# The passage from the filter stage to the first token tile: store position, last frequency pairs, and the order and banks at the first last stage

## Chip, cores and metric

The kernel runs on one core of one Trainium2 chip, as one launch. The metric is the device time of that launch in microseconds (us); lower is better. Times given as positions ("at 294.16") are microseconds from the start of the span of one profiled execution.

## What is computed

The reference is a long convolution with a small learned filter, a gate, and a maxout feed-forward layer on the result:

```python
h_mlp = np.maximum(pos_emb @ w1, 0.0) @ w2            # 12544 x 128, filter
h_filt = h_mlp * exp(-0.01 * pos)
u = x * v                                              # 4 x 12544 x 128
y = irfft(rfft(u, 2S) * rfft(h_filt, 2S), 2S)[:, :S]   # per channel
a = (x * y).reshape(50176, 128)
h = maximum(maximum(a @ w1m, a @ w2m), a @ w3m)        # 128 -> 768
out = h @ w_out                                        # 768 -> 128
```

All arrays are float32 on the chip (the feed-forward weights arrive as 64-bit floats and are converted there). There are B = 4 samples of S = 12544 positions and D = 128 channels.

## The kernel before

**Transforms as products.** A sequence of 12544 positions is seen as 98 blocks (NB) of 128. The Fourier transform of each channel is done in two stages of small matrix products. The first stage works on "units": a unit is four channels, and there are 32 of them per sample. `u_first` multiplies a unit's turned data by a table (32 matmuls, line 413), ScalarE copies one half of the result out of PSUM into a buffer `high` (line 422), and VectorE writes sum and difference of the two halves into `spec` (line 424). The second stage works on 45 "pairs" of frequencies (NK = 45, pairs 0 to 44): a product with the second table, a multiplication by the filter's spectrum, and the product of the inverse transform, whose result goes to DRAM (`zd`).

**Token tiles.** The rest of the inverse transform runs tile by tile. A tile is four block positions, 392 tokens; a sample has 32 tiles (NT). `t_load` brings a tile's data back from `zd` to `zt` and the matching x to `xT`; `t_sums` makes sum and difference of its halves (line 703); `t_last` does the last product (32 small matmuls through line 156) and VectorE multiplies by x into `gt` (line 724). Then for six blocks of 128 hidden units `up` does two products into a ring of three PSUM banks called `hbanks`, ScalarE applies relu (line 734), VectorE takes the maximum (line 737), and `down` accumulates the output product two steps later. The third maxout branch was folded into the other two beforehand; the fold product is `lin` (line 1085 copies it out).

**Order.** The program order of every engine is written out by hand: each engine and each DMA queue works its own list in order, and the framework adds the waits that buffers and data need. SyncE's queue issues nearly all loads; POOL (GpSimd) issues the stores of the filter and of the output.

**The stage before the passage** is the loop at line 1038 over s, from 0 to 47. In one turn it starts pair s, makes the filter of pair s-1 (`s_filter`, lines 1007 and 1012: a product, and a copy into a buffer `ht`, of which there are two), stores it for later samples (`s_store`, line 1018: two DMAs on POOL's queue), multiplies pair s-2 by its filter and makes sum and difference for the inverse product (`g_re`, `g_im`, `g_unfold`: lines 549, 553, 554, 561), and does the inverse product of pair s-3 (`g_third`, stored by line 574). At s = NK two pairs, 43 and 44, are handled in one turn: both are multiplied, then both unfolded, and the add of pair 43 is on POOL (`apart`).

**The passage.** Units 0 to 5 of the second sample (unit 0 at s = 45, unit 1 behind the loop, units 4 and 5 only turned there) use PSUM banks of the stage that is ending; `banks_of` lists them in order. Behind the loop the fold products run (`folding`), `lin` is copied out, the old pools are closed, and the new ones open: three banks of the up ring, two double banks `cps` for everything else ("pairs" in the code), one bank for the output. The first tile of sample 0 then runs in this order: loads of tiles 0 and 1, `t_sums` of tile 0 on VectorE, `u_first(2)`, `t_last` of tile 0, `u_first(3)`, and the first `up`. From there the products of the second sample's transform are put between the tiles' products, by slots that a planner (`conv_steps`) assigns.

Of the kernel before, what the change touches and what calls it, by code (L numbers as in the profile page):

```python
# [10 lines left out]
FP32 = mybir.dt.float32  # L11
I32 = mybir.dt.int32
U16 = mybir.dt.uint16
ALU = mybir.AluOpType
ACTF = mybir.ActivationFunctionType
PSUM = bass.MemoryType.PSUM
P = 128
# [74 lines left out]
def kernel(  # L92
# [15 lines left out]
    nc = tc.nc  # L108
    NG, _, _, B, NB = x.shape
# [4 lines left out]
    NK = N1 // 2  # L114
# [286 lines left out]
                t[0:NB, 4 * h:4 * h + 4].rearrange("n s p -> n (s p)").rearrange(  # L401
                    "n (s t r) -> n s r t", s=8, r=2))

    def u_first(u, i0=0, n=4):


        t = uts[u] if i0 + n < 4 else uts.pop(u)
        ps = state["bank"]()[:, 0:256 * n]
        at = 4 * u + i0
        for i in range(n):  # L410
            for h in range(2):
                for c in range(2):
                    nc.tensor.matmul(  # L413
                        ps[64 * c:64 * c + 64, 256 * i + h * N1:256 * i + (h + 1) * N1],
                        t[:, 2 * ((at + i) % 8) + h].rearrange("n r t -> n (r t)"),
                        f1q[:, h, c * N1:(c + 1) * N1],
                        start=(i % 2 == 0 and h == 0), stop=True, skip_group_check=True)
        v = ps.rearrange("p (s m) -> p s m", m=256)[:, :, 0:2 * N1].rearrange(
            "p s (h k) -> p h k s", h=2)
        high = cvp.tile([P, n, D], FP32, tag="eo", name="high", bufs=2)  # L420
        high = high[:, :, 0:N1].rearrange("p s k -> p k s")
        nc.scalar.copy(high, v[:, 0])  # L422
        for a, op in enumerate((ALU.add, ALU.subtract)):
            nc.vector.tensor_tensor(out=spec[:, :, a, at:at + n], in0=v[:, 1], in1=high, op=op)  # L424

    def w_load(x):
        w = wp.tile([P, 2, 2, 2, 64], FP32, tag="w", name="wt")
# [123 lines left out]
    def g_im(g, apart=False):  # L551
        xt, xs = xts[g], xss.pop(g)
        nc.vector.tensor_tensor(out=xs[:], in0=xs[:], in1=hts.pop(g)[:, 1], op=ALU.mult)
        (nc.gpsimd if apart else nc.vector).tensor_tensor(
            out=xt[:], in0=xt[:], in1=xs[:], op=ALU.add)
# [112 lines left out]
    def t_load(b, i):  # L668
        zt = hp.tile([N1, 2, 512], FP32, tag="zt", name="zt", bufs=2)
        for c in range(2):  # L670
            if b == 0:
                nc.sync.dma_start(
                    zt[NK * c:NK * c + NK],
                    zd[b].rearrange("(g a) c t f -> g a c t f", a=2)[
                        :, :, c, 2 * i:2 * i + 2, :].rearrange("g a t f -> g a (t f)"))
                continue
            q, j = divmod(i, NT // 2)
            for a in range(2):
                nc.sync.dma_start(
                    zt[NK * c:NK * c + NK, a].rearrange("g (t f) -> g t f", t=2),  # L680
                    zd[b].rearrange("(g a) c t q f -> g a c t q f", a=2)[
                        :, a, c ^ (a & q), 2 * j:2 * j + 2, q, :])
        zts[b, i] = zt[:, 0], zt[:, 1]
        if i % 2:
            return
        xT = hp.tile([D, 2, 4, NB], FP32, tag="xT", name="xT", bufs=2)
        for c in range(GC):
            nc.sync.dma_start(xT[c * NG:(c + 1) * NG].rearrange("d i p n -> d (i p) n"),
                              x[:, 4 * i:4 * i + 8, c, b, :])
        xTs[b, i], xTs[b, i + 1] = xT[:, 0], xT[:, 1]  # L690
# [3 lines left out]
    def t_sums(i, eng=nc.gpsimd, parts=(0, 1)):  # L694
        z0, z1 = zts[i]
        if 0 in parts:
            evens_[i] = hp.tile([N1, 512], FP32, tag="even", name="even", bufs=2)
        even = evens_[i]
        for a, (out, op) in enumerate(((even[:], ALU.add), (z1, ALU.subtract))):
            if a not in parts:  # L700
                continue
            if i[0] == 0 or i[1] < NT // 2:
                eng.tensor_tensor(out=out, in0=z0, in1=z1, op=op)
            else:
                nc.vector.scalar_tensor_tensor(out=out, in0=z1, scalar=sign_t[:, 0:1], in1=z0,
                                               op0=ALU.mult, op1=op)
        if 1 in parts:
            zts[i] = evens_.pop(i)[:], z1

    def t_last(i):  # L710
        zt = zts.pop(i)
        ps = state["bank"]()
        own = i[0] == B - 1 and i[1] > 1
        g = (lp if own else hp).tile([D, 4, NB], FP32, tag="g", name="gt", bufs=4 if own else 3)
        y = ps[:, 0:N].rearrange("d (p n) -> d p n", p=4)

        h = NB // 2
        for s in range(4):
            for a in range(2):
                halves_mm(y[:, s, a * h:a * h + h], zt[a][:, s * D:(s + 1) * D],  # L720
                          f4p[:, i[0] > 0 and i[1] >= NT // 2, a, :], s == 0 and a == 0, True)
        y = y.rearrange("d p (a m) -> d p m a", a=2)
        xT = xTs.pop(i)
        nc.vector.tensor_tensor(out=g[:].rearrange("d p (m a) -> d p m a", a=2), in0=y,
                                in1=xT.rearrange("d p (m a) -> d p m a", a=2),
                                op=ALU.mult)
        gs[i] = g
# [180 lines left out]
    for f in range(0, FO, 4):  # L908
        quad([hs[:, f + i] for i in range(4)], (f1h[:, 0], f1h[:, 1]), specH[:, :, :, f:f + 4])
        u, k = divmod(f // 4, 4)  # L910
# [36 lines left out]
    gps = pro.enter_context(tc.tile_pool(name="gps", bufs=2, space=PSUM))  # L947
    sps = pro.enter_context(tc.tile_pool(name="sps", bufs=1, space=PSUM))
    def banks_of():
        for _ in range(2):  # L950
            yield gps.tile([P, 512], FP32, tag="g", name="ps1")[:]
        both = sps.tile([P, 1024], FP32, tag="h", name="ps1")
        for h in range(2):
            yield both[:, 512 * h:512 * h + 512]
        for pool, tag in ((cps, "cv"), (gps, "g")):
            yield pool.tile([P, 512], FP32, tag=tag, name="pst")

    free = banks_of()

# [56 lines left out]
    def s_store(g):  # L1016
        for c in range(2):
            nc.gpsimd.dma_start(
                hd[g, 64 * c:64 * c + 64],
                hts[g][64 * c:64 * c + 64, c].rearrange("p k q d -> p (k q d)"))  # L1020
# [17 lines left out]
    for s in range(NK + 3):  # L1038
        if s < NK:
            ws[s, 0] = wf[s]  # L1040
            s_second(s)
            if s + 1 < NK:
                s_minus(s + 1)
            g_second(s)
            wf.pop(s)
            if s + 3 < NK:
                wf[s + 3] = load_dir(s + 3, 0)
        if 1 <= s <= NK:
            g_swap(s - 1)
            s_filter(s - 1)  # L1050
        if s >= 3:
            ws[s - 3, 1] = wi.pop(s - 3)
            g_third(s - 3)
            if s < NK:
                wi[s] = load_dir(s, 1)
        ready = [g for g in {NK: (s - 2, s - 1)}.get(s, (s - 2,)) if 0 <= g and s <= NK]
        for g in ready:
            s_store(g)
            g_re(g)
            g_im(g, g == NK - 2)  # L1060
        for g in ready:
            g_unfold(g)
        if s < NK:
            g_butterfly(s)

        if s in muls:
            u_mul(muls[s])
        if s in turns:
            u_turn(turns[s])
        if s in loads:  # L1070
            u_load(1, loads[s])
        if s == NK:
            unit(0)
            pl = sps.tile([P, 512], FP32, tag="pl", name="pl")
        if s == NK + 1:
            for f in range(2):
                folding(f)
# [40 lines left out]
    for n, (b, i) in enumerate(tiles[:LAST]):  # L1118
        if i == 0:
            plan, pairs_from = plans[b]  # L1120
        if n == 0:
            t_load(*tiles[0])
            t_load(*tiles[1])
            t_sums(tiles[0], nc.vector)
            u_first(2)
            t_last(tiles[0])
            u_first(3)
        for f in range(NF):

            if i < NT - 2:  # L1130
                if f == 0:
                    t_load(*tiles[n + 2])
            elif i == NT - 1 and f < 2 and n + 1 + f < len(tiles):
                t_load(*tiles[n + 1 + f])
            turn_ = i == NT - 1
            if f == 4 and n + 1 == LAST:
                t_sums(tiles[n + 2], nc.vector)
            h = up((b, i), f)
            for a in range(2):
                if f == plan[i][a]:  # L1140
                    t_sums(tiles[n + 1],
                           nc.vector if turn_ or i * NF > pairs_from else nc.gpsimd, (a,))
            late.append(((b, i), f, h))
            if len(late) > 2:
                down(*late.pop(0))
            if f == plan[i][2]:
                t_last(tiles[n + 1])
            if f == 5 and n + 1 == LAST:
                t_last(tiles[n + 2])
            run(besides.pop(n * NF + f, ()))  # L1150
# [97 lines left out]
```

## Time and profile before

| | |
|---|---|
| median of three runs | 2289.66 us (2287.26 to 2293.03) |
| the profiled execution | 2287.31 us, span 2285.5 us |
| TensorE (PE) busy | 2258.4 us, 99% |
| VectorE (DVE) busy | 1558.0 us, 68% |
| ScalarE (ACT) busy | 1173.6 us, 51% |
| GpSimd (POOL) busy | 871.6 us, 38% |
| mean granted TensorE clock | 0.997 |
| first `up` product of tile 0 | 313.67 us |

The profile is of one execution on the chip. PE is TensorE's matmuls, PEld its weight loads; SPq and POOLq are the queues in which SyncE and GpSimd issue DMAs. A busy share over the whole span mixes stages with different limits, so the passage, some 30 us near position 300, is read by itself below.

### The profile page before, as it was taken

The numbers are of one execution on the slowest core, as the hardware profiler recorded it, in microseconds if no ns is written. First come the engines' busy times: TensorE is split into PE (matmuls) and PEld (weight loads), VectorE is DVE, ScalarE is ACT, GpSimd is POOL, SyncE is SP. The second block draws the span as 40 slices with busy tenths as digits, with TensorE's granted clock in tenths as the row PEclk, the third lists the DMA queues.
The fourth block names the chain that finished last, engine by engine and source line by source line (L and its number), as shares of the span: only waits on it lengthen the run. The fifth ranks groups of instructions, "written<-read, shape, count | busy, mean of one in ns | idle before, by whom it ended". The sixth has DMA issues, their size and how long they took to land.

```text
span 2285.5 us, 68501 instructions
## 1 busy us (share of the span) xinstructions
PE 2258.4 (99%) x27855; PEld 1381.6 (60%) x27855; DVE 1558.0 (68%) x2853; ACT 1173.6 (51%) x2124; POOL 871.6 (38%) x1088
## 2 busy tenths in 40 slices
PE   8999989999999999999999999999999999999998
PEld 7988866655555556655555556655555546666665
DVE  5588956667788757657878756667878854544443
ACT  2688844456666534456666534456666622222222
POOL 2044424323332333423333334413333326666666
PEclk9999999999999999999999999999999999999999
DMA  7778979799989779879999789879999832222221
GB/s 188 182 233 271 302 169 179 147 216 241 237 220 241 190 169 177 162 182 254 238 232 240 207 162 188 155 183 246 233 239 237 204 86 56 56 67 65 62 56 22
DMA packets 473270, 411.03 MB, mean 180 GB/s; under 512 B 327866, under 2 KB 374427, under 8 KB 472955
## 3 DMA queue, kind: packets, MB, share of 16 engines
q1 hardware_dynamic: 445954, 329.48, 63.8%
q0 software_dynamic: 26288, 75.47, 11.1%
q8 instruction: 219, 3.59, 0.7%
q10 hardware_dynamic: 712, 1.70, 0.3%
q14 instruction: 97, 0.79, 0.1%
HBM read 262.84 MB, written 84.67 MB: 152 GB/s over the span
## 4 chain that ended last, share of the span: by engine, by line
PE 96%; DMA 2%; DVE 1%; issue 1%; ACT 0%; SPq 0%; POOL 0%; POOLq 0%; DVEq 0%; ACTq 0%
PE hps L156 44%; PE ops L156 19%; PE ops L797 6%; PE cps L413 5%; PE cps L156 4%; PE ps L156 3%; PE cps L467 3%; PE ps L165 3%; PE cps L477 3%; PE sps L1007 2%; PE gps L989 2%; PE last L156 1%; DMA hd<-ht 1%; PE pst L366 1%; PE pm L328 1%
## 5 line engine op out<-in xcount | busy, mean ns | idle before, releaser
L156 PE MATMUL hps<-gt,w_sb 128*64 128x392 f32 x6144 | 1150.4, 494 | 0.0
L734 ACT ACTIVATE hid<-hps 128x392 f32<-128x392 f32 x768 | 383.7, 500 | 697.6 <-PE hps L156 680.8
L156 PEld LDWEIGHTS hps<-gt,w_sb 128*64 128x64 f32 x6144 | 432.6, 137 | 419.6 <-issue 384.0
L737 DVE TENSOR_TENSOR hid<-hid,hps 128x392 f32<-128x392 f32 x768 | 427.8, 557 | 332.4 <-PE hps L156 322.2
L156 PE MATMUL ops<-hid,wo_sb 128*64 128x392 f32 x2304 | 480.5, 492 | 0.0
L519 POOL TENSOR_TENSOR cb<-cb,xs 128x512 f32<-128x512 f32 x135 | 173.6, 1286 | 463.4 <-DVE xs L516 346.1
L156 PEld LDWEIGHTS ops<-hid,wo_sb 128*64 128x64 f32 x2304 | 172.8, 137 | 206.4 <-issue 197.8
L424 DVE TENSOR_TENSOR spec<-cps,high 128x360 f32<-128x360 f32 x188 | 141.0, 790 | 127.8 <-ACT high L422 127.0
L492 DVE TENSOR_TENSOR cb<-cps,eo 128x512 f32<-128x512 f32 (+1 forms) x288 | 175.1, 649 | 73.9 <-ACT eo L489 73.9
L752 POOL DMA_DIRECT2D out_dram<-ot x96 | 75.1, 783 | 345.5 <-ACT ot L750 298.0
L507 ACT ACTIVATE xs<-cb 32x512 f32<-32x512 f32 x270 | 169.5, 628 | 20.4 <-DVE cb L492 11.5
L422 ACT COPY high<-cps 128x360 f32<-128x360 f32 x94 | 75.0, 798 | 182.5 <-PE cps L413 149.1
L508 ACT COPY xs<-cb 32x512 f32<-32x512 f32 x270 | 166.3, 616 | 3.2
L413 PEld LDWEIGHTS cps<-f1q,uT 98*64 98x64 f32 x3008 | 131.9, 138 | 29.8 <-issue 23.8
L523 DVE TENSOR_TENSOR xs<-cb 128x256 f32<-128x256 f32 x270 | 140.8, 566 | 9.1 <-POOL cb L519 8.9
L413 PE MATMUL cps<-f1q,uT 98*64 98x90 f32 x3008 | 136.3, 242 | 3.2 <-DVE uT L397 1.5
L382 POOL COPY planes<-ut 128x784 uint16<-128x784 uint16 x90 | 76.4, 849 | 153.5 <-DVE ut L361 153.5
L500 POOL DMA_DIRECT2D zd<-cb x135 | 92.5, 685 | 64.5 <-DVE cb L492 56.9
L156 PEld LDWEIGHTS cps<-f4p,even 90*64 90x64 f32 x1568 | 90.8, 138 | 34.8 <-issue 32.8
L156 PE MATMUL cps<-f4p,zt 90*64 90x49 f32 x1568 | 97.4, 222 | 0.1
L821 POOL DMA_DIRECT2D out_dram<-o x128 | 77.4, 610 | 49.6 <-DVE o L814 47.9
L156 PE MATMUL cps<-f4p,even 90*64 90x49 f32 x1568 | 96.1, 220 | 0.0
(135 smaller groups left out, 3140.6 us busy)
## 6 DMA issues: line engine op xcount, KB each, us to landing
ht<-hd SPq DMA_DIRECT2D x264, 256.0 KB, 6.9
wt<-wq_const SPq DMA_DIRECT2D x144, 256.0 KB, 6.3
zd<-cb POOLq DMA_DIRECT2D x135, 256.0 KB, 6.1
zt<-zd SPq DMA_DIRECT2D x384, 90.0 KB, 3.1
sq<-spec SPq DMA_DIRECT2D x264, 128.0 KB, 7.0
ut<-in_xr_dram SPq DMA_DIRECT2D x128, 196.0 KB, 3.9
ut<-in_vr_dram SPq DMA_DIRECT2D x128, 196.0 KB, 4.1
xT<-in_x_dram SPq DMA_DIRECT2D x256, 98.0 KB, 3.3
```

The lines of the kernel that those rows point to most:

```text
L156: nc.tensor.matmul(out[64 * h:64 * h + 64], lhsT[:, 64 * h:64 * h + 64], rhs, start=start, stop=stop, skip_group_check=True)
L413: nc.tensor.matmul(ps[64 * c:64 * c + 64, 256 * i + h * N1:256 * i + (h + 1) * N1], t[:, 2 * ((at + i) % 8) + h].rearrange("n r t -> n (r ...
L424: nc.vector.tensor_tensor(out=spec[:, :, a, at:at + n], in0=v[:, 1], in1=high, op=op)
L492: nc.vector.tensor_tensor(out=cb[:, a, lo:hi], in0=ps[:, lo:hi], in1=eo[:, lo:hi], op=op)
L500: nc.gpsimd.dma_start(zd[b][2 * z:2 * z + 2].rearrange("k c t a f -> (k c t) a f"), zss.pop(z))
L507: nc.scalar.mul(xs[at:at + 32], xt[at + 32:at + 64], -1.0)
L508: nc.scalar.copy(xs[at + 32:at + 64], xt[at:at + 32])
L519: nc.gpsimd.tensor_tensor(out=xts[g], in0=xts[g], in1=xs[:], op=ALU.add)
L523: nc.vector.tensor_tensor(out=ab[:, q], in0=y[:, 0], in1=y[:, 1], op=(ALU.subtract, ALU.add)[q])
L734: nc.scalar.activation(h[:], pa[:, 0:N], Relu)
L737: nc.vector.tensor_tensor(out=h[:], in0=h[:], in1=pb[:, 0:N], op=ALU.max)
L797: nc.tensor.matmul(ps[64 * c:64 * c + 64, 0:H2], w, rhs[:, H2 * c:H2 * c + H2], start=start, stop=True, skip_group_check=True)
```

## The change

Four things are altered; the work computed is the same.

- The stores of filters 42 and 43 are issued one turn of the loop sooner: at s = 43 those of 41 and 42, at s = 44 that of 43, at s = 45 that of 44.
- At s = 45 pair 43 is multiplied, added and unfolded, and then pair 44; both adds are on VectorE.
- The list of banks gives unit 1's two halves two different tiles (the filter's double tile and one of the two `gps` banks) instead of two halves of one tile.
- `u_first` is split into `u_products` (products and the copy to `high`) and the two VectorE operations that it returns as a function. At tile 0 the order becomes: loads, unit 2 whole, products of unit 3, `t_sums`, `t_last` in the next bank of the up ring, and then unit 3's two VectorE operations.

```diff
-    def u_first(u, i0=0, n=4):
+    def u_products(u, i0=0, n=4):
...
         nc.scalar.copy(high, v[:, 0])
-        for a, op in enumerate((ALU.add, ALU.subtract)):
-            nc.vector.tensor_tensor(out=spec[:, :, a, at:at + n], in0=v[:, 1], in1=high, op=op)
+
+        def both():
+            for a, op in enumerate((ALU.add, ALU.subtract)):
+                nc.vector.tensor_tensor(out=spec[:, :, a, at:at + n], in0=v[:, 1], in1=high,
+                                        op=op)
+        return both
+
+    def u_first(*args):
+        u_products(*args)()
...
-    def t_last(i):
+    def t_last(i, bank=None):
         zt = zts.pop(i)
-        ps = state["bank"]()
+        ps = bank or state["bank"]()
...
     def banks_of():
-        for _ in range(2):
-            yield gps.tile([P, 512], FP32, tag="g", name="ps1")[:]
-        both = sps.tile([P, 1024], FP32, tag="h", name="ps1")
-        for h in range(2):
-            yield both[:, 512 * h:512 * h + 512]
-        for pool, tag in ((cps, "cv"), (gps, "g")):
-            yield pool.tile([P, 512], FP32, tag=tag, name="pst")
+        for pool, tag, n in ((gps, "g", 1), (gps, "g", 1), (sps, "h", 2), (gps, "g", 1),
+                             (cps, "cv", 1), (gps, "g", 1)):
+            yield pool.tile([P, 512 * n], FP32, tag=tag, name="ps1")[:, 0:512]
...
         ready = [g for g in {NK: (s - 2, s - 1)}.get(s, (s - 2,)) if 0 <= g and s <= NK]
+        for g in {NK - 2: (s - 2, s - 1), NK - 1: (s - 1,), NK: (s - 1,)}.get(s, (s - 2,)):
+            if 0 <= g and s <= NK:
+                s_store(g)
         for g in ready:
-            s_store(g)
             g_re(g)
-            g_im(g, g == NK - 2)
-        for g in ready:
+            g_im(g)
             g_unfold(g)
...
             t_load(*tiles[1])
+            u_first(2)
+            third = u_products(3)
             t_sums(tiles[0], nc.vector)
-            u_first(2)
-            t_last(tiles[0])
-            u_first(3)
+            t_last(tiles[0], next(hbanks))
+            third()
```

## Prediction

> **What bounds the kernel now.** I read the busy shares first. TensorE is busy 2258.4 of 2285.5 us, so only about 27 us of the span are TensorE idle. The mean granted clock is 0.997. Then I asked for TensorE's waits. From 320 to 1850 us they sum to 1.5 us, so a change can pay only in the start, in the passage from the filter stage to the first token tile, or at the end. The diff touches the passage. From 287 to 315 us TensorE is busy 20.67 of 28 us at a mean clock of 0.82. The timeline of TensorE, cut to the instructions that waited there (start, length, instruction, in brackets the idle time before it and what ended it):
>
> ```profile
> 287.67 1.10 PE L1007 MATMUL sps<-w2x,G 64*64 64x128 f32 x32 [0.79 <-ACT ht L1012]
> ...
> 294.16 1.97 PE L156 MATMUL ps<-ab,wt 128*64 128x128 f32 x16 [3.12 <-DVE ab L561]
> ...
> 301.97 0.84 PE L413 MATMUL ps<-f1q,uT 98*64 98x90 f32 x16 [1.34 <-DVE spec L424]
> ...
> 307.02 1.46 PE L413 MATMUL cps<-f1q,uT 98*64 98x90 f32 x32 [0.36 <-ACT lin L1085]
> ...
> 311.06 2.61 PE L413 MATMUL cps<-f1q,uT 98*64 98x90 f32 x32 [1.38 <-DVE spec L424]
> ```
>
> In order: the last filter product; inverse product of pair 43; second half of unit 1; unit 2; unit 3. Sixteen 128-wide matmuls take 1.09 us at 288.70 but 1.97 us at 294.16, and unit 3 takes 2.61 us against unit 2's 1.46: the clock. By windows (columns: window, length, then busy time and count of PE, PEld, DVE, ACT and POOL, then granted clock, DMA share, GB/s):
>
> ```profile
> 294.00:301.00 7.00, 6.20 (x54) 5.15 (x54) 2.59 (x9) 1.79 (x5) 0.00 (x0) 0.51 0.28 92
> ...
> 311.00:315.00 4.00, 3.94 (x39) 3.16 (x41) 0.87 (x2) 0.90 (x2) 2.48 (x3) 0.57 0.67 153
> ```
>
> Next, why pair 43 waited. VectorE, then POOL:
>
> ```profile
> 288.26 0.68 DVE L553 TENSOR_TENSOR xs<-xs,ht 128x512 f32<-128x512 f32 x1
> 291.75 0.69 DVE L549 TENSOR_TENSOR xt<-xt,ht 128x512 f32<-128x512 f32 x1 [2.81 <-ACT ht L1012]
> ...
> 293.69 1.42 DVE L561 TENSOR_TENSOR ab<-xt 128x256 f32<-128x256 f32 x4
> ```
>
> ```profile
> 284.10 1.04 POOL L1018 DMA_DIRECT2D hd<-ht  x2 [2.06 <-ACT ht L1012]
> 287.91 1.05 POOL L1018 DMA_DIRECT2D hd<-ht  x2 [2.77 <-ACT ht L1012]
> 289.03 1.27 POOL L554 TENSOR_TENSOR xt<-xt,xs 128x512 f32<-128x512 f32 x1
> ```
>
> Pair 43 has its filter at 287.65. Its sum is done on POOL at 290.30, but VectorE unfolds it only at 293.69, behind all of pair 44. Pair 44 waits for a filter buffer: the copy at 290.70 had to wait until the store of filter 42 landed. The chain of waits (start, length, what):
>
> ```profile
> 284.61 5.99 DMA hd<-ht
> ...
> 290.70 1.02 ACT ht L1012
> ...
> 300.13 2.18 DMA zd<-zs
> ```
>
> From 300.13 the chain goes on through the store of the last inverse result, its reload (landed 307.15) and the sums to the first up product at 313.67.
>
> **What the Trainium skill says.** "TensorE: Matmul & The Clock Gate", Part 1, has the array at half clock after an idle window of about 3.4 us, back at full after a busy one, with windows that run freely. The trace agrees: 3.12 us idle, then clock 0.50 until after 300.6 us. "PSUM — Partial Sum Buffer", section on bank collisions, says to guard PSUM by bank. Unit 1's halves lie in different banks but in one tile, and the second waits 1.34 us for the first's readers: here the wait comes from the tile, and two tiles remove it. "DMA: Bandwidth & Descriptors", Anatomy of one DMA, gives about 2.0 us of fixed cost; the lone store at 300.13 took 2.2 us, so an earlier issue moves it whole.
>
> **The change, part by part.**
>
> 1. Stores. Those of filters 42 and 43 move an iteration up: four DMA issues of 0.53 us on POOL's queue, passing nothing there, since POOL's last other step (the negation at 280.10) stays ahead. Both began 0.30 us after the copy they need (283.80 to 284.10, 287.61 to 287.91), with POOL idle before. So nothing is won; filter 44 is still copied at 290.70. Nothing lost either.
>
> 2. Last pairs. POOL's add (1.27) goes, VectorE's (0.69) comes, and pair 43 is unfolded before pair 44 begins. VectorE is idle from 288.94 to 291.75, which covers it: add 288.97 to 289.66, unfold to 290.45. TensorE ends unit 0 at 291.04, so pair 43 runs at once: 3.12 us of wait gone. Late next is pair 44: multiplies and add 291.75 to 293.76 unchanged, its unfold now first, 293.79 to 294.50. Between lie two transposes and a fold product, about 1.0 us. Pair 44's product goes from 294.2 and ends at **T' = 295.3** at full clock or 296.1 at half, where before T = 299.43. Its output buffer is free when the store of 292.23 lands (3.2 us: 295.4), about when it is needed. Gain at T: 3.3 to 4.1 us.
>
> 3. Banks. Unit 1's second half goes to another tile, freed by unit 0's adds (about 295.5): 1.34 us gone. The folding from unit 1's end (302.81) to the end of `lin` (306.97) keeps its 4.16 us. So **L'** = T' + 1.41 + 4.16 = 300.9 at full clock; at half, T' + 2.82 + 4.16 = 303.1.
>
> 4. Order at tile 0. Unit 3's product follows unit 2's; the last stage stands in a bank of the up products, so it waits for no adds of unit 2; unit 3's adds follow. But on VectorE unit 2's two adds now stand ahead of the tile's sums; before, the sums filled the wait for unit 2's copy. From L': copy of unit 2 starts at +1.67, its adds end at +3.95 (as before), sums (0.69 + 0.69) at +5.35, last stage ends 1.08 later as it did (308.61 to 309.69), product with x 0.56: first up product at **U' = L' + 7.15**. The reload, landing 7.7 us after T', is no longer last: 303.0 against adds that end at 304.9. Before, U was L + 6.70, with 1.15 of clock in unit 3. So this part gives back 0.45, or 1.6 at equal clocks.
>
> Sum: full clock, U' = 308.05 against 313.67, 5.6 us; half, 310.25, 3.4 us. The quiet stretch from L' + 2.8 to U' holds only 1.3 us of TensorE work, so half clock after it is as likely as not: up to 1.7 us (half of a window that the page puts at 3.4; before, the up products lost 0.5). That takes 0.35 on average. I weigh the clocks 55 to 45: 0.55 x 5.2 + 0.45 x 3.0 = 4.2; **4.3 us** taken, as the sums could move up if the clock is full. The extremes of this case are 2.2 and 6.1.
>
> 5. Later. One more bank in the up ring turns it by one place: nothing, since each up still takes the next of three. Unit 3's adds (1.49) after the first product with x hold a pair bank and a copy buffer not needed before unit 5. The ring's first banks are free by then. But the last stage now ends 0.75 us ahead of U', where it ended 4.0 ahead of U; its end frees the buffer for tile 2's load, and behind that load on SP's queue stand four x loads and eight unit loads. VectorE's multiply of unit 7 needs data that landed 10.3 us after the last stage's end: now U' + 9.6, done at U' + 10.2. TensorE waits only from about U' + 11.0 (the maximum of the fourth up product has 1.8 us in hand). Costed at nothing, by 0.8 us.
>
> The profiled execution took 2287.31 us around its span of 2285.5; the median of the three runs is 2289.66. Taking 4.3 off each gives 2283.0 and **2285.4**.
>
> **Rivals.** *Supply binds* (0.15): the SP queue above. In absolute time the last stage ends only 0.2 to 2.4 us sooner (307.3 to 309.5 against 309.69). If the loads pace TensorE, the gain is that, 2288. For: DMA share near 1.0 from 315 on. Against: no engine waited for a unit load before. *Clock stays full* (0.15): gain 6.1 at most against the profiled execution, and up to 8 against the median, which stands 2.35 above it: 2282 to 2284. *The clock stays low from 292 to past the first ups* (0.10), the other side: idle 292.5 to 293.75 triggers it, and folding with many transposes fails to lift it. L' = 294.2 + 1.97 + 2.82 + 6.5 (its 3.3 us of work doubled, 0.9 waits) = 305.5, unit 2 adds 1.2, U' = 313.9 and the ups lose 1.2 more: 1.4 us slower, 2291. It decides where the clock between 292 and 308 falls under about 0.6. *The change does nothing in its first part*: argued above, inside every case. The forecast has 0.60.
>
> **Numbers.** Runs of this kernel differ by 5.8 us among three, and 0.3% is 6.9 us, about what can be told from no change. The range 2281.5 to 2289.5 takes in the forecast's extremes, supply and most of the full-clock case. Faster by over 0.3% needs a median under 2282.8: half of the full-clock case and a share of the forecast's, 0.18. Slower by over 0.3% needs something not seen here: 0.03.
>
> **What would show it.** Right: pair 43's product at about 291.0 without a wait; no wait in unit 1; the stores still 0.3 us after their copies; filter 44's copy near 290.7; unit 2's adds ahead of the sums; the first up near 308 to 311. Wrong: a filter copy or store that moved by over 1 us; a wait of VectorE for unit loads near 315 followed by TensorE waits; a sum of TensorE's waits after 320 above 3 us.

## The result

The changed kernel takes 2284.69 us in the median of 22 runs (2281.04 to 2287.29), the kernel before 2289.15 in 22 runs beside them: 4.46 us less. The ratio is 0.998, 95% interval 0.9974 to 0.9987, that is 3.0 to 6.0 us. The forecast was 2285.4. The gain is within the 0.3% that the forecast called no change, but clear of noise. One execution of a later set of 20, at 3354 us and a clock of 0.654, is left out of every figure below.

The profiled execution of the changed kernel has by chance the same span as that of before, 2285.5 us: at 2287.29 us it is the slowest of its 22, while that of before, 2287.31, lies 1.8 us under its median. Its stages ahead of the passage ran 3.2 us later, so positions of the two traces can't be compared as they stand. I count from a mark ahead of every edit but the stores': **F**, the start of the last filter product (287.67 before, 290.91 after). The stores of filters 42 and 43 stand where they stood from F: 3.57 us ahead of it and 0.24 behind it, in both traces. TensorE after the change, mostly its waits (start, length, instruction, idle before and what ended it; L156 is the line of a helper, and the trace counts each float32 matmul of the program as two):

```profile
290.91 1.10 PE L1010 MATMUL sps<-w2x,G 64*64 64x128 f32 x32 [0.79 <-ACT ht L1015]
...
296.76 0.44 PE L156 MATMUL pl<-wo_sb,w1t 128*64 128x128 f32 x4 [0.88 <-ACT w1t L974]
297.61 1.17 PE L156 MATMUL ps<-ab,wt 128*64 128x128 f32 x16 [0.40 <-issue]
298.60 1.41 PE L413 MATMUL ps<-f1q,uT 98*64 98x90 f32 x32
...
304.22 2.70 PE L413 MATMUL cps<-f1q,uT 98*64 98x90 f32 x64 [0.36 <-ACT lin L1089]
308.78 0.32 PE L156 MATMUL hps<-f4p,even 90*64 90x49 f32 x4 [1.85 <-DVE even L710]
309.50 0.32 PE L156 MATMUL hps<-f4p,zt 90*64 90x49 f32 x4 [0.40 <-DVE zt L710]
...
311.19 2.88 PE L156 MATMUL hps<-gt,w_sb 128*64 128x392 f32 x8 [0.67 <-DVE gt L731]
...
320.72 1.41 PE L413 MATMUL cps<-f1q,uT 98*64 98x90 f32 x32
```

The first up product and unit 5's products in the kernel before:

```profile
313.39 2.11 PE L156 MATMUL hps<-gt,w_sb 128*64 128x392 f32 x8
...
320.50 1.44 PE L413 MATMUL cps<-f1q,uT 98*64 98x90 f32 x32
```

The 3.12 us ahead of pair 43 and the 1.34 us inside unit 1 (298.60, now 32 matmuls in one piece) are gone. The first up product starts at F + 20.28, where it started at F + 25.72. (The 313.67 of the table before, F + 26.0, is the end of the products ahead of it; its first matmul starts at 313.39.) But it now takes 2.88 us for 8 matmuls that take 1.54 in the fill kernel below, at full clock. By windows (length, busy time and count of PE, PEld, DVE, ACT, POOL, then the granted clock, DMA share, GB/s):

```profile
294.00:310.00 16.00, 11.85 (x194) 9.07 (x192) 8.16 (x18) 8.12 (x19) 1.05 (x2) 1.00 0.62 161
310.00:318.00 8.00, 7.33 (x66) 4.55 (x64) 3.10 (x5) 1.65 (x3) 2.76 (x3) 0.57 0.72 169
```

The half clock of 294 to 301 is gone; that behind the first last stage has grown from 3.4 to 6.8 us. VectorE and POOL:

```profile
292.22 0.69 DVE L561 TENSOR_TENSOR xt<-xt,xs 128x512 f32<-128x512 f32 x1
293.01 0.76 DVE L568 TENSOR_TENSOR ab<-xt 128x256 f32<-128x256 f32 x2
294.95 0.69 DVE L556 TENSOR_TENSOR xt<-xt,ht 128x512 f32<-128x512 f32 x1 [1.18 <-ACT ht L1015]
...
306.69 1.44 DVE L426 TENSOR_TENSOR spec<-cps,high 128x360 f32<-128x360 f32 x2 [5.46 <-ACT high L422]
308.04 0.68 DVE L710 TENSOR_TENSOR even<-zt 90x512 f32<-90x512 f32 x1
```

```profile
287.34 1.05 POOL L1021 DMA_DIRECT2D hd<-ht  x2 [2.37 <-ACT ht L1015]
291.15 1.05 POOL L1021 DMA_DIRECT2D hd<-ht  x2 [2.76 <-ACT ht L1015]
295.21 1.05 POOL L1021 DMA_DIRECT2D hd<-ht  x2 [3.02 <-ACT ht L1015]
```

Pair 43 is unfolded (293.01) before pair 44 has its filter (294.95). The sums (308.04) begin when unit 2's adds end. The chain of waits shows what pair 43 hangs on now:

```profile
288.01 6.27 DMA wt<-wt_const
294.29 0.14 issue
294.42 1.09 PE ps L156 x16
```

Its inverse table landed 0.14 us before it ran. In run 7, where no load stands in the chain ahead of it, the product starts 1.25 us after the start of unit 0's products; here it is 1.55.

### The profile page after: what moved, and what is told of

Read it like the earlier page. It is cut to its first block, busy times and chain, and to the rows that moved or that the text cites. A ratio compares the mean times of both kernels' runs of the same rounds, so it can differ in the third digit from the quotient of the medians.

```text
span 2285.5 us, 68498 instructions
## 1 busy us (share of the span) xinstructions
PE 2258.2 (99%) x27855; PEld 1376.8 (60%) x27855; DVE 1558.6 (68%) x2854; ACT 1175.3 (51%) x2124; POOL 871.8 (38%) x1087
## 4 chain that ended last, share of the span: by engine, by line
PE 96%; DMA 1%; DVE 1%; ACT 1%; issue 0%; POOL 0%; POOLq 0%; ACTq 0%; DVEq 0%; SPq 0%
PE hps L156 44%; PE ops L156 19%; PE ops L804 6%; PE cps L413 5%; PE cps L156 4%; PE cps L474 3%; PE ps L156 3%; PE ps L165 3%; PE cps L484 3%; PE sps L1010 2%; PE gps L992 1%; PE last L156 1%; DMA hd<-ht 1%; PE pst L366 1%; PE pm L328 1%; PE pw L156 1%
## 5 line engine op out<-in xcount | busy, mean ns | idle before, releaser
L156 PE MATMUL hps<-gt,w_sb 128*64 128x392 f32 x6144 | 1151.1, 495 | 0.7 <-DVE gt L731 0.7
L156 PEld LDWEIGHTS hps<-gt,w_sb 128*64 128x64 f32 x6144 | 430.9, 137 | 422.3 <-issue 393.4
L156 PE MATMUL ops<-hid,wo_sb 128*64 128x392 f32 x2304 | 479.9, 492 | 0.0
L156 PEld LDWEIGHTS ops<-hid,wo_sb 128*64 128x64 f32 x2304 | 171.8, 137 | 207.4 <-issue 207.4
L413 PEld LDWEIGHTS cps<-f1q,uT 98*64 98x64 f32 x3008 | 131.4, 138 | 29.3 <-issue 26.5
L156 PEld LDWEIGHTS cps<-f4p,even 90*64 90x64 f32 x1552 | 89.6, 138 | 35.0 <-issue 34.2
L156 PE MATMUL cps<-f4p,zt 90*64 90x49 f32 x1552 | 96.3, 222 | 0.0
L156 PE MATMUL cps<-f4p,even 90*64 90x49 f32 x1552 | 95.0, 220 | 0.0
```

The costliest lines, as they stand in the source:

```text
L156: nc.tensor.matmul(out[64 * h:64 * h + 64], lhsT[:, 64 * h:64 * h + 64], rhs, start=start, stop=stop, skip_group_check=True)
L413: nc.tensor.matmul(ps[64 * c:64 * c + 64, 256 * i + h * N1:256 * i + (h + 1) * N1], t[:, 2 * ((at + i) % 8) + h].rearrange("n r t -> n (r ...
```

## Experiments

**How they are read.** For each trace I give the passage, from F to the start of unit 5's products (line 413; from 320 to 1850 us TensorE waits 1.5 us in all, before and after), and the rest of the span behind it. "Half clock" is the time at half clock from the first last stage on: twice the shortfall of the granted clock, summed over windows of 1 us.

| kernel | F | unit 5 | passage | half clock | rest | ratio, 95% interval |
|---|---|---|---|---|---|---|
| before | 287.67 | 320.50 | 32.83 | 3.4 | 1965.0 | |
| before again | 287.45 | 321.54 | 34.09 | 3.4 | 1965.6 | 0.9999, 0.9989 to 1.0010 |
| changed | 290.91 | 320.72 | 29.81 | 6.8 | 1964.8 | 0.9980, 0.9974 to 0.9987 |
| changed again | 288.04 | 317.33 | 29.29 | 6.8 | 1964.6 | 0.9984, 0.9977 to 0.9991 |
| pairs undone | 287.90 | 321.46 | 33.56 | 3.4 | 1964.7 | 0.9997, 0.9988 to 1.0005 |
| banks undone | 287.79 | 319.70 | 31.91 | 6.8 | 1964.8 | 0.9997, 0.9988 to 1.0006 |
| order undone | 287.40 | 317.21 | 29.81 | 6.8 | 1964.8 | 0.9984, 0.9978 to 0.9991 |
| stores undone | 290.00 | 319.56 | 29.56 | 6.8 | 1964.8 | 0.9981, 0.9974 to 0.9987 |
| pairs alone | 286.35 | 314.54 | 28.19 | 3.4 | 1965.1 | 0.9983, 0.9976 to 0.9990 |
| fill | 288.53 | 314.54 | 26.01 | 0 | 1966.4 | 0.9990, 0.9983 to 0.9997 |
| filter buffer | 287.88 | 316.59 | 28.71 | 6.8 | 1965.0 | 0.9991, 0.9984 to 0.9997 |
| old order, fill | 287.66 | 317.04 | 29.38 | 3.4 | 1964.8 | 0.9984, 0.9976 to 0.9992 |
| fill, loads | 287.25 | 314.27 | 27.02 | 0 | 1965.8 | 0.9987, 0.9979 to 0.9995 |
| combined | 288.70 | 314.68 | 25.98 | 0 | 1966.0 | 0.9978, 0.9968 to 0.9988 |

Each ratio is to executions of the kernel before made beside those of that row. The medians of these sets lie between 2286.83 and 2289.15, so a median says something only next to its own set. The intervals are 3.0 to 4.8 us wide, so they separate only the larger effects; the traces carry the finer ones, but each is one execution.

**Theory and rivals.** Theory: the gain starts at pair 43, the banks add the wait in unit 1, the stores are worth nothing, the order at tile 0 gives time back. Rivals: the order and its bank make the gain; the stores do.

**1. Pairs undone.**

```diff
-            g_im(g)
-            g_unfold(g)
+            g_im(g, g == NK - 2)
+        for g in ready:
+            g_unfold(g)
```

> Changed kernel, but pairs 43 and 44 multiplied and unfolded together again, with pair 43's add on POOL. Measure: time from the last filter product's start (F) to the start of unit 5's products, 32.8 us in the profile before, 29.8 in the changed one. Theory (the gain starts at pair 43): pair 43's product waits about 3 us again and starts near F + 6.5, the clock falls, L' is near F + 18.7, the first up product near F + 26: passage 32 to 33, median near 2289. Rival (the order at tile 0 and its bank make the gain): passage stays near 30, median near 2285.

Measured: passage 33.56, ratio 0.9997: the gain is gone. The trace is 0.7 us longer than the first of the kernel before (and 0.5 shorter than its second). TensorE, VectorE and POOL show what is new in it:

```profile
295.91 1.98 PE L156 MATMUL ps<-ab,wt 128*64 128x128 f32 x16 [4.63 <-DVE ab L568]
```

```profile
293.69 1.82 DVE L561 TENSOR_TENSOR xt<-xt,xs 128x512 f32<-128x512 f32 x1
```

```profile
292.62 1.04 POOL L1021 DMA_DIRECT2D hd<-ht  x2 [3.44 <-ACT ht L1015]
293.68 1.27 POOL L561 TENSOR_TENSOR xt<-xt,xs 128x512 f32<-128x512 f32 x1
```

With the stores at their new place the last store stands ahead of POOL's add, which so waits for the last filter copy. It then runs beside VectorE's add, which takes 1.82 us instead of 0.69. So in this trace the stores' new place costs time as long as the add is on POOL; this run isn't a clean undo of one part. Run 5 is.

**2. Banks undone.** `banks_of` as before.

> Changed kernel, but unit 1's halves in one tile again. Theory: the second half waits about 0.7 to 1.4 us again, and all behind it moves by that: passage 30.5 to 31.2, median near 2286. Rival (the reload of the tile comes last anyway, so the banks are worth nothing): the wait is there, but the first up product stands where it stood, F + 20.3; median near 2284.7.

Measured: passage 31.91, 2.1 longer, ratio 0.9997. The wait is back, and later there is a second cost:

```profile
297.60 0.84 PE L413 MATMUL ps<-f1q,uT 98*64 98x90 f32 x16 [1.34 <-DVE spec L426]
...
309.04 0.45 PE L156 MATMUL hps<-f4p,zt 90*64 90x49 f32 x4 [1.51 <-DVE zt L710]
```

VectorE's second sum of tile 0 took 1.80 us (307.18), since POOL did the sum of tile 1 beside it (307.17 to 308.43). That 1.1 us belongs to the collision in this execution, the other 1.3 to the banks (together 2.4 against 2.1; two traces of the changed kernel differ by 0.5). The first up product stands at F + 23.65, so the rival falls, but the passage is longer than the 31.2 that I expected.

The executions leave more to explain than the trace. The median, 2286.98, is 2.15 us below its own set's 2289.13, but the ratio is that of run 1: the gain is gone, and the interval doesn't meet the changed kernel's. With the new order the old banks thus cost some or all of the gain. With the old order they cost none that shows (run 5). Why the two go together is open.

**3. Order undone.** The five lines at tile 0 as before.

> Changed kernel, but sums, unit 2, last stage, unit 3 in the order of before, with the last stage in a double bank. Theory (the new order gives time back): the first up product starts later, near F + 21.2, with unit 3's products ahead of it, but TensorE's quiet stretch is shorter; if the clock stays full the passage is shorter than the changed kernel's 29.8 by up to 2, median 2283 to 2285. Rival (the order is a gain of its own): passage 31 or more, median 2286 or more.

Measured: passage 29.81, to the hundredth that of the changed kernel; ratio 0.9984. The order is worth nothing that shows. The quiet stretch is there too: the sums wait for the reload, TensorE is idle 2.92 us ahead of the last stage, and the clock falls for two windows as in the changed kernel:

```profile
304.84 0.34 PE L156 MATMUL cps<-f4p,even 90*64 90x49 f32 x4 [2.92 <-DVE even L710]
```

```profile
305.00:312.00 7.00, 6.62 (x72) 5.10 (x72) 3.90 (x6) 1.28 (x2) 2.76 (x3) 0.51 0.55 134
```

Both my expectation of a shorter passage and the rival's of a longer one fail. In this order the passage hangs on the reload, and so on the last inverse result's store ahead of it. That store took 3.2 us here and 2.2 in run 5 (2.1 to 3.5 over all traces), so one trace can't tell 0.45 us from nothing.

**4. Stores undone.** The stores in the loop over `ready` as before, ahead of the multiplications.

> Changed kernel, but the stores at their old places in the loop. Theory: nothing; the stores start 0.3 us after the filter copies they wait for, the last filter's copy starts 3.0 us after F, median within 1.5 us of 2284.7. Rival (the earlier stores are what frees the filter buffer): the last copy starts over 1 us later, median 2286 or more.

Measured: passage 29.56, ratio 0.9981. The stores start 0.3 us behind their copies, and the last filter's copy at F + 2.8 (F + 3.0 in the changed kernel). The rival falls.

**5. Pairs alone,** on the kernel before:

```diff
             g_re(g)
-            g_im(g, g == NK - 2)
-        for g in ready:
+            g_im(g)
             g_unfold(g)
```

> Kernel before with one edit: pairs 43 and 44 one after the other, both adds on VectorE. Theory: pair 43's product starts 3 us earlier (near F + 3.5 instead of F + 6.5), unit 1's second half still waits 1.34 us, passage 30.5 to 31.9 against 32.8 before and 29.8 in the changed kernel, median 2286 to 2287. Rival (the parts work only together): passage over 32.3, median 2288.5 or more.

Measured: passage 28.19, ratio 0.9983. One edit of the four gives all that the whole change gives:

```profile
286.35 1.10 PE L1007 MATMUL sps<-w2x,G 64*64 64x128 f32 x32 [0.79 <-ACT ht L1012]
...
289.68 1.09 PE L156 MATMUL ps<-ab,wt 128*64 128x128 f32 x16
...
295.98 0.84 PE L413 MATMUL ps<-f1q,uT 98*64 98x90 f32 x16 [1.33 <-DVE spec L424]
...
314.54 1.45 PE L413 MATMUL cps<-f1q,uT 98*64 98x90 f32 x32
```

Pair 43's product starts at F + 3.33 without a wait. The wait of 1.33 us in unit 1 is there, and yet the first up product starts at F + 20.18, as in the changed kernel. The passage is even 1.6 shorter, which is what the clock would give: this execution had 3.4 us of half clock where that had 6.8, and half of the 3.4 us more is 1.7.

**6. Fill.** Does that half clock cost what it seems to?

```diff
-            t_last(tiles[0], next(hbanks))
+            mine, fill = next(hbanks), next(hbanks)
+            for _ in range(6):
+                halves_mm(fill[:, 0:P], lin[:], lin[:], True, True)
+            t_last(tiles[0], mine)
+            for _ in range(2):
+                halves_mm(fill[:, 0:P], lin[:], lin[:], True, True)
```

> Changed kernel with extra TensorE work in the quiet stretch: 12 matmuls of 128 columns on constant data ahead of the first last stage (about 1.6 us) and 4 behind it, into a bank of the up ring that the next up product overwrites; nothing reads them. Theory (the half clock after the quiet stretch takes back about 3 us): the clock stays at 1.0 past the first up products, passage 26.5 to 27.5 instead of 29.8, median near 2282. Rival (the ups are slow for another reason, or the clock falls all the same): passage 29.5 to 30.5, median 2284.5 to 2285.5.

Measured: the clock stays at 1.00 through 308 to 316, and the passage is 26.01, 3.8 less than in the changed kernel.

```profile
307.98 1.54 PE L156 MATMUL hps<-gt,w_sb 128*64 128x392 f32 x8 [0.22 <-DVE gt L731]
```

Not all of it is the fill's. The store of filter 42 landed sooner in this execution (3.6 us after its issue in the median of its two halves, 4.4 in the changed kernel's first trace), so the last filter's copy started at F + 1.75 without waiting, and the first up product at F + 19.45 instead of F + 20.28. From there to unit 5 it is 6.56 us against 9.53: the fill's share is about 3.0. In the trace the theory holds. But the ratio is 0.9990, and the rest is 1.6 us longer than the changed kernel's. VectorE, waiting for a unit's data:

```profile
316.94 0.57 DVE L361 TENSOR_TENSOR ut<-ut 128x392 f32<-128x392 f32 x1 [2.84 <-DMA ut<-in_vr_dram]
318.38 0.57 DVE L361 TENSOR_TENSOR ut<-ut 128x392 f32<-128x392 f32 x1 [0.88 <-DMA ut<-in_vr_dram]
```

This is the prediction's supply rival, at its place.

The rest takes back 1.6 of the 3.8 us; why the ratio shows none of the other 2.2 can be seen in part from the clock of all executions. Its mean was 0.9975 over the changed kernel's 22, 0.9980 over the 19 of its second set, and 0.9984 over the fill kernel's 21. At half speed that is 5.8, 4.7 and 3.7 us of TensorE's time over the span. So in the mean the fill saves 1.0 to 2.1 us of clock, about one window, and not the two of the changed kernel's traces.

**7. Filter buffer.** The last filter's copy goes in two halves to two buffers of the forward tables:

```diff
+        if g == NK - 1:
+            own = [lwp.tile([P, 2, 2, D], FP32, tag="w0", name="ht") for _ in range(2)]
```

> Changed kernel, but the last filter's copy goes in two halves to two buffers of the forward tables that are free by then, so that it waits for no store. Theory (pair 44 is bound by the landing of filter 42's store): the copy starts about F + 1.7 instead of F + 3.0, pair 44's multiplies with it; the end of pair 44's product moves by 0.5 to 1.2 us, as the tables for it land near F + 6; the reload moves likewise, but the fold chain too, passage 28.6 to 29.3, median 2283.5 to 2284.2. Rival (pair 44 is bound by ScalarE's queue or the table): no move of pair 44's product, median 2284.7.

Measured: the copy starts at 289.63, F + 1.75, and pair 44's product at 293.62, F + 5.74 instead of F + 6.70; passage 28.71, ratio 0.9991. In the changed kernel's trace pair 44 was bound by the store's landing, and 0.6 to 1.1 us reach unit 5 (29.3 or 29.8 against 28.7). Run 6 agrees: where that store happened to land early, pair 44's product started at F + 5.86 without this edit. The ratio shows no gain over the changed kernel.

**8 to 10. Loads.** Is it SyncE's queue that makes VectorE wait? Run 8 has the old order at tile 0 with a fill of 18 matmuls (36 in the trace) ahead of the first last stage. Run 9 is run 6 with tile 2's load behind the unit loads; run 10 adds the copy of run 7.

```diff
-                if f == 0:
+                if f == 0 and n > 0:
                     t_load(*tiles[n + 2])
...
             run(besides.pop(n * NF + f, ()))
+            if n == 0 and f == 0:
+                t_load(*tiles[2])
```

> Order at tile 0 as in the kernel before (pairs and banks as changed), with 18 matmuls of 128 columns on constant data, which nothing reads, between unit 2's products and the first last stage. Theory (at full clock the two orders differ by little, and the old one frees the tile buffer for the loads sooner): passage 26.5 to 27.5 where the changed order with fill had 26.0; from unit 5 to the end 1964.8 to 1965.1 us as in the kernel before, not 1966.4. Rival (the late loads come from the fill, not from the order): VectorE waits for unit loads here as well, and 1966 or more behind unit 5.

> The fill kernel (changed order), but the load of tile 2 stands behind the unit loads of slot 0 on SyncE's queue, so that these do not wait for the first last stage. Theory (the 2.8 us wait of VectorE for a unit load came from SyncE's queue): that wait is gone, TensorE keeps its passage of 26.0, and the rest from unit 5 to the end is 1964.8 to 1965.1 instead of 1966.4; median 1 us or more below the fill kernel's. Rival (the transfers themselves were slow): the wait stays above 1.5 us.

> Changed kernel with the fill, the loads of tile 2 behind the unit loads, and the last filter's copy in buffers of its own. Theory: the gains add: passage 25.0 to 25.6, rest 1965, 4 to 5 us below the changed kernel in the same call. Rival (the earlier filter copy is lost on the reload of the tile): passage 26.

Run 8: passage 29.38 where 26.5 to 27.5 was expected, one window of half clock, a wait of 0.6 us of VectorE for a unit load, rest 1964.8. The fill was too short for this order's gap (0.98 us idle were left), so it tells little. Run 9: the wait of 2.84 is gone, as the theory has it, but the rest is still 1965.8, with 0.73 us of TensorE waiting for a unit's turned data at 440.31, and the ratio, 0.9987, is not told from the fill kernel's 0.9990. Its passage, 27.02, is longer than run 6's since the last filter's copy waited again (F + 3.11). Run 10: passage 25.98, rest 1966.0, and a wait at a third place:

```profile
393.79 0.57 DVE L361 TENSOR_TENSOR ut<-ut 128x392 f32<-128x392 f32 x1 [3.28 <-DMA ut<-in_vr_dram]
```

The three kernels with passages of 26 to 27 all lose 1.0 to 1.6 us in the rest against the changed kernel, at different places. So the queue's order explains the first wait only. That the stage's transfers are the limit fits a DMA share near 1.0, but isn't shown: the kernel before has 0.96 to 1.06 from 315 to 360 too, and loses nothing. The gains of run 10 didn't add up as expected: its passage is 1.0 shorter than run 9's but no shorter than run 6's, which had the early copy by chance, and its median, 2282.42, is 1.2 us below the changed kernel's 2283.60 beside it, not 4 to 5. Its ratio, 0.9978, is the lowest, and its interval covers the changed kernel's: a version that is faster is not established.

**11 and 12. Both kernels again.**

> The changed kernel once more, on the same chip as the three above. Expected: 3 to 6 us below the kernel before; from unit 5 to the end 1964.8; the passage 26.5 to 30, by how many windows of half clock fall behind the first last stage in this execution.

> The kernel before once more, unchanged, for a second trace of its passage and for what the comparison gives between identical kernels. Expected: ratio 1.000 within its interval; passage 32 to 35 us; pair 43's wait 3.1 us; the half clock behind it in whole windows of about 3.4 us. If the median of the kernel before is above the first profiled execution because of such windows, a trace with a lower mean clock shows more of them, in the passage or elsewhere.

Measured: 29.29 and 34.09. The second trace of the kernel before has the same wait ahead of pair 43,

```profile
293.97 1.97 PE L156 MATMUL ps<-ab,wt 128*64 128x128 f32 x16 [3.15 <-DVE ab L561]
```

but three stretches of half clock in the passage (6.8 us from 293.0, 3.4 from 303.2, 3.4 from 313.4) where the first had two. The gain from trace to trace is thus 3.0 (32.83 to 29.81) to 4.8 (34.09 to 29.29), which covers the 4.46 of the medians.

## Why the prediction was right

**Parts 1 to 4, the sum.** Counted from F, by the full-clock line of the sum:

| mark | predicted | measured |
|---|---|---|
| pair 43's product | F + 3.4 | F + 3.5 |
| end of pair 44's product (T') | F + 7.6 | F + 7.9 |
| end of `lin` (L') | F + 13.2 | F + 13.3 |
| first up product (U') | F + 20.4 | F + 20.3 |
| gain at the first up product | 5.6 | 5.7 (5.4 by the first matmul's start) |

Stores: nothing, as costed; run 4 (with the add still on POOL they would have cost, run 1). Pairs: all of the net gain; runs 1 and 5. Banks: 1.34 us in the trace of run 2 and up to the whole gain by its ratio, but nothing where the order is the old one (run 5 does without them). The prediction has no such tie between the two parts. Order: predicted to give back 0.45; run 3 shows none, either way.

Two of the prediction's sums are off without harm. Part 4's items add up to L' + 6.99, not 7.15, and 7.0 was measured. In the rival with the low clock, 3.3 us of work doubled and 0.9 of waits are 7.5, not 6.5, so it should have stood 1 us slower.

**The term that was mis-sized is the clock behind the quiet stretch.** I put its average at 0.35 us lost (half of 1.7, less the 0.5 lost before) and its worst at 1.7, one window. It was two windows, 6.8 us at half clock or 3.4 us of work, in both traces of the changed kernel, and in four of the others. From the start of the first up product to unit 5 the changed kernel takes 9.53 us (before 7.11, with the fill 6.56). So of the 5.4 us gained at the first up product 2.4 were lost again by unit 5, and the profiled gain was 3.0.

The median's gain is nearer to the forecast, because neither trace is the typical one. The changed kernel's is its slowest of 22, and in the mean over its executions the clock cost 1.0 to 2.1 us more than with the fill, about one window (run 6). The kernel before varies more: run 12 has 1.3 us more in its passage than the execution that I worked from, and over the 58 executions beside runs 1 to 4 a mean clock lower by 0.001 went with 1.4 us more time (correlation 0.76). The total therefore came out at 4.46 against 4.3 with one part of it by luck.

**Two smaller terms.** The reload landed 8.9 us behind T', not 7.7: the inverse result waited for its buffer, and its store took 3.2 us instead of 2.2. It cost nothing, since unit 2's adds ended later still (308.0 against 307.7). And pair 43's product hung on its table, a limit that the prediction doesn't have; it held the product up by some 0.3 us, and in run 9 TensorE waited 0.25 us for it. That cost nothing either: pair 44, which comes later, waits for its own filter.

**The supply rival** costs nothing to TensorE in the changed kernel, as forecast: from unit 5 to the end it takes 1964.8 us, before 1965.0. In its second trace VectorE waits 0.78 us for a unit load. Where the passage was under 28 us the rest grew by 1.0 to 1.6 us (runs 6, 9, 10). All three have the fill, so whether the early passage or something else about them does it is not shown. The rival with the clock low from 292 on didn't occur: there it stayed at 1.00 to 310.

## To carry to other kernels

When a stall is taken away, find the next quiet stretch on TensorE and charge what follows it with whole windows of half clock. In the traces here it was one where TensorE was busy right through the first, and two where that window had gaps. This can eat nearly half of what was won. Ask of a profiled execution where it stands among the others of its kernel before its clock is taken for typical. Before four edits are made at one place, run the one that removes the longest wait alone: here it was the whole gain. And count positions from a mark ahead of the edits, since two executions of the same stages differed by 3 us at that mark.

## What the runs showed of the hardware

The clock falls for whole windows: every stretch at half clock in these traces, but for the last one at the program's end, lasts 3.41 or 6.83 us. The Trainium skill, "TensorE: Matmul & The Clock Gate", Part 1, gives a window of 3413 ns; the traces agree with it. It has the clock return after at least one busy window, and fall after an idle one.

How busy is enough can be read from the traces. Cut the time at the changes of clock into windows of 3.41 us and add up TensorE's busy time in each. Around the first last stage:

| kernel, start of the first window | busy us, clock | busy us, clock | busy us, clock | busy us, clock |
|---|---|---|---|---|
| before, from 307.76 | 1.95, full | 3.41, half | 3.41, full | |
| pairs alone, from 302.73 | 2.18, full | 3.41, half | 3.41, full | |
| changed, from 307.04 | 1.27, full | 2.74, half | 3.41, half | 3.41, full |
| order undone, from 301.60 | 0.49, full | 3.03, half | 3.41, half | 3.41, full |
| fill, from 305.05 | 2.29, full | (the clock stays full) | | |

In the passages of the 11 traces that have half clock there, it ended behind every window with 3.12 us or more of busy time (15 windows) and went on behind every one with 3.08 or less (9). This is no sharp limit: at the program's start a window of 2.78 ended it (run 6). From full clock it fell behind windows with 0.35 to 2.18 us busy and never, in any trace, behind 2.19 or more; between 1.4 and 2.18 both occurred. So a window need not be idle, and no single wait need be as long as one: the longest ahead of the fall in the changed kernel is 1.85 us. In the changed kernel the first window at half clock holds the 0.67 us wait ahead of the first up product, and a second followed. In the kernel before TensorE was busy right through it. Where the windows lie against the work differs from one execution to the next.

Two elementwise additions, one on VectorE and one on POOL at the same time, took 1.80 (run 2) and 1.82 us (run 1) on VectorE, where one alone takes 0.69; it ended 0.55 us after POOL's had ended. The tile stages of the changed kernel's trace show the same: VectorE's 128x256 sums of `cb` take 0.41 us alone (216 of them) and 1.34 in the median beside an addition of POOL (54). Operations that read one input from PSUM do not change: the maximum of line 744 takes 0.56 us alone (517) and beside POOL (251).
